# Layer-norm statistics of the first rows split over VectorE, ScalarE and GpSimd, other work moved behind or ahead

## The chip, the core and the metric

The kernel runs on one core of a Trainium2 chip. The time is device microseconds of one execution; a kernel is judged by the median of several. One more execution is profiled, and its trace gives what every engine did and when: TensorE (PE, its weight loads PEld), VectorE (DVE), ScalarE (ACT), GpSimd (POOL), SyncE (SP), which issues most of the DMAs.

## The reference

The input x has 2048 rows of 640. Each row is normalised (mean and variance over 640, eps 1e-5) to xn. Two branches read xn, and the result is x + s * g:

```python
x = A_x
xn = _layernorm(x, axis=-1)
s = _A_ref(xn, A_wq, A_wk, A_wv, A_wo, A_beta)   # attention, see below
g = _silu(_B_ref(xn, B_w_gate, B_w_up, B_w_down)) # (sigmoid(xn wg) * (xn wu)) wd
return x + s * g
```

The attention has 32 heads of 20 columns. The rows are cut in 4 segments of 512. Within a segment there is causal softmax attention; beside it stands a read from a memory matrix that sums phi(k) v over the earlier segments (phi(t) = t+1 for t > 0, else exp(t)), divided by its normaliser. Each head mixes the two by a gate sigmoid(beta), and wo projects the result. The gated branch has 1536 inner columns.

## The kernel before, in words

The whole program is written in one order by hand: each engine runs its instructions in the order in which the Python code emits them. A planner places the later work in 20 slots a segment; `at` and `later` give it due times. The change touches `startup`, which runs ahead of the slots, and what it calls.

In `startup` (L573) the first segment's 512 rows are taken in 4 blocks of 128 rows. Their DMAs are issued on SP first (`x_first`, L137), two blocks to a tile `xt2`, mixed with the two halves of Wv; Wk and Wq follow, then blocks of the next segment and gate weights. For each block:

- `ln_stats` (L227): two `bn_stats` and one `bn_aggr` on VectorE give mean and variance; GpSimd adds eps and raises to the power -0.5 (L241, L242), which gives `rstd`.
- `ln_norm` (L248): VectorE writes `xn` = (x - mean) * rstd. In the first segment TensorE transposes it in five pieces into a PSUM tile `pT` (L260) and ScalarE copies that to `xnT` (L261). In the second segment a DMA issued on SP transposes (L263).

`v_tile(0, j, half)` (L356) multiplies block j's part of `xnT` by one half of Wv in five matmuls into `psv`; ScalarE copies the result to `va` (L280). Six of the eight value tiles of the first segment stand in `startup`. `k_chunk` and `q_chunk` (L282, L314) need all four blocks of `xnT`; each is five matmuls of 512 columns, copied by ScalarE, five of each. `warm` (L568) issues matmuls of the identity with itself, whose result nobody reads, ahead of the first transposes (WARM = 40) and between the first and the second (10).

All these PSUM tiles (wps, pT, psv, psk, psq, gp, up) come from one ring of three buffers (`dtile`, L114): the fourth tile waits until the first is read.

GpSimd's other work in `startup`: it makes `ident`, fills `KT[0]` with ones (L575), then behind the value tiles fills the ones columns of `va` (`v_ones`, L192), builds the indicator `nInd` (`make_ind`, L196) and fills `KT[1]` and `KT[2]` (L593, L596). Key chunks read `nInd` at L305.

Keys and queries are staged to DRAM and come back in another layout: `stage_out` (L308) writes, `relay` (L271) issues four DMAs on SP that read the rows of half the heads into `KT` or `QT`. `relay(0, 1, Ks, KT)` (L630) brings the first segment's second half of key rows; the scores of slot 10 and later read them. `load_glu(i, which)` (L161) loads a third of the gate or up weights.

Of the kernel before, what the change touches and what calls it, by code (L numbers as in the profile page):

```python
# [9 lines left out]
P = 128  # L10
S = 2048
D = 640
# [17 lines left out]
ACT = mybir.ActivationFunctionType  # L30
ALU = mybir.AluOpType
# [18 lines left out]

NU = len(UNITS)
NSLOT = NG // 2 * NU
WARM = 40
FIRST = 0.45
PASS = [0.41, 0.41, 0.41, 0.2, 0.61]
R = NSLOT / 24
# [3 lines left out]
def kernel(  # L60
# [14 lines left out]
    nc = tc.nc  # L75
# [3 lines left out]
    cpool = ctx.enter_context(tc.tile_pool(name="const", bufs=1))  # L79
# [3 lines left out]
    lnp = ctx.enter_context(tc.tile_pool(name="ln", bufs=2))  # L83
    xpool = ctx.enter_context(tc.tile_pool(name="xpool", bufs=2))
# [44 lines left out]
    st = [dict() for _ in range(NSEG)]  # L129
# [31 lines left out]
    def load_glu(i, which):  # L161
        w, src = ((Wg, B_w_gate), (Wu, B_w_up))[which]
        nc.sync.dma_start(w[i][:], src[:, i * L:(i + 1) * L].rearrange("(c p) n -> p c n", p=P))
# [11 lines left out]

    nhalf = cpool.tile([P, 2], F32, name="nhalf")
    nc.gpsimd.memset(nhalf[:], -0.5)
    ident = cpool.tile([P, P], BF, name="ident")
    nc.gpsimd.memset(ident[:], 0.0)
    nc.gpsimd.affine_select(out=ident[:], in_=ident[:], compare_op=ALU.not_equal, fill=1.0,  # L180
# [6 lines left out]
    KT = [cpool.tile([P, 4, L], BF, name=f"KT{i}") for i in range(3)]  # L187
# [4 lines left out]
    def v_ones(a, b):  # L192
        for i in range(a, b):
            nc.gpsimd.memset(V[i][:, :, DH:VW], 1.0)
# [32 lines left out]
    def ln_stats(n, p, i0=0, i1=2):  # L227
        s = st[n]
        x = s[f"x{p}"]
        if i0 == 0:  # L230
            s[f"mv{p}"] = lnp.tile([P, 2, 2], F32, name="mv")
            s[f"rstd{p}"] = lnp.tile([P, 2], F32, name="rstd")
        mv, rstd = s[f"mv{p}"], s[f"rstd{p}"]
        for i in range(i0, i1):
            bs = lnp.tile([P, 2, 6], F32, name="bs")
            nc.vector.bn_stats(bs[:, 0, :], x[:, i, 0:HB])
            nc.vector.bn_stats(bs[:, 1, :], x[:, i, HB:D])
            nc.vector.bn_aggr(mv[:, i, :], bs[:])

        def root():  # L240
            nc.gpsimd.tensor_scalar(rstd[:, i0:i1], mv[:, i0:i1, 1], EPS, None, op0=ALU.add)  # L241
            nc.gpsimd.tensor_tensor(rstd[:, i0:i1], rstd[:, i0:i1], nhalf[:, i0:i1], op=ALU.pow)  # L242
        if n <= 1:
            root()
        else:
            later(0.6, root)

    def ln_norm(n, p, i):  # L248
# [4 lines left out]
        nc.vector.tensor_scalar(xn[:], s[f"x{p}"][:, i, :], s[f"mv{p}"][:, i, 0:1], s[f"rstd{p}"][:, i:i + 1],  # L253
                                op0=ALU.subtract, op1=ALU.mult)
        j = 2 * p + i
        dst = s["xnT"][:, :, j * P:(j + 1) * P]
        if n == 0:
            pT = dtile([P, DC, P], BF, "pT")
            for c in range(DC):
                nc.tensor.transpose(pT[:, c, :], xn[:, c * P:(c + 1) * P], ident[:])  # L260
            nc.scalar.copy(dst, pT[:])  # L261
        elif n == 1:
            nc.sync.dma_start_transpose(dst, xn[:])  # L263
        else:
            later(0.7, lambda: nc.sync.dma_start_transpose(dst, xn[:]))
# [5 lines left out]
    def relay(n, half, src, dst):  # L271
        rows = src[n % 2].rearrange("(g r d) n -> r d g n", r=4, d=DH)
        for r in range(4):
            nc.sync.dma_start(half_tile(dst, n, half)[32 * r:32 * r + DH, :, :], rows[r][:, 4 * half:4 * half + 4, :])
# [81 lines left out]
    def v_tile(n, j, half):  # L356
        s = st[n]
        ps = dtile([P, HB], F32, "psv")
        for k in range(DC):
            nc.tensor.matmul(ps[:], lhsT=s["xnT"][:, k, j * P:(j + 1) * P],  # L360
                             rhs=W["v"][:, k, half * HB:(half + 1) * HB],
                             start=(k == 0), stop=(k == DC - 1))
        va = V[4 * (n % 2) + j]
        evacuate(va[:, half * 16:(half + 1) * 16, 0:DH], ps[:].rearrange("p (h e) -> p h e", e=DH))
# [203 lines left out]
    def warm(count):  # L568
        ps = dtile([P, L], F32, "wps")
        for i in range(count):  # L570
            nc.tensor.matmul(ps[:, 0:P], lhsT=ident[:], rhs=ident[:], start=True, stop=True)

    def startup():  # L573
        warm(WARM)
        nc.gpsimd.memset(KT[0][:], 1.0)  # L575
        ln_stats(0, 0, 0, 1)
        ln_stats(0, 0, 1, 2)
        ln_norm(0, 0, 0)
        warm(10)
        ln_stats(0, 1, 0, 1)  # L580
        ln_norm(0, 0, 1)
        v_tile(0, 0, 0)
        ln_stats(0, 1, 1, 2)
        v_tile(0, 1, 0)
        ln_norm(0, 1, 0)
        v_tile(0, 0, 1)
        ln_norm(0, 1, 1)
        v_tile(0, 2, 0)
        v_tile(0, 1, 1)
        v_tile(0, 2, 1)  # L590
        v_ones(0, 4)
        make_ind()
        nc.gpsimd.memset(KT[1][:], 1.0)  # L593
        for c in range(DC):
            k_chunk(0, c)
        nc.gpsimd.memset(KT[2][:], 1.0)  # L596
        stage_out(0, 0, Ks, KT, "k5")
        for c in range(DC):
            q_chunk(0, c)
            if c == 0:  # L600
                stage_out(0, 1, Ks, KT, "k5")
                relay(0, 0, Ks, KT)
            elif c == 2:
                stage_out(0, 0, Qs, QT, "q5")
            if c < 2:
                ln_stats(1, 0, c, c + 1)
        make_bd()
        v_ones(4, 8)
        take(1)
        q_bound(0)  # L610
        relay(0, 0, Qs, QT)
        stage_out(0, 1, Qs, QT, "q5")
        c_in(0, (0,))
        load_glu(1, 0)
        load_glu(1, 1)
# [130 lines left out]
    n = NSEG - 1  # L746
# [39 lines left out]
```

## Time and profile before

| what | us |
|---|---|
| median of three runs | 339.98 |
| lowest and highest run | 338.81, 341.98 |
| profiled execution | 339.46 |
| span of its trace, first to last instruction | 337.70 |
| granted TensorE clock | 0.999 |
| first warm-up matmul starts | 1.45 |
| first key matmul starts | 12.42 |
| first scores start | 32.59 |

A timeline line reads: start and length in us, engine, source line, operation, output <- input, shapes, how many such instructions in a row were merged; in brackets the idle time of the engine ahead of it and what ended that. A line of a stage reads: the stage, its length, then busy time and number of instructions of each engine, the granted clock, the mean share of 16 DMA engines that was busy, and GB/s. Busy time of TensorE counts warm-up matmuls too.

### The profile page before, as it was taken

Reading aid. Unit: us, or ns where it says so; the run is one execution under the profiler, and the core shown is the slowest. Engines: PE = TensorE matmul, PEld = TensorE weight load, DVE = VectorE, ACT = ScalarE, POOL = GpSimd, SP = SyncE. Lnnn points to the kernel's source line nnn. Section 1 sums busy time; section 2 is a strip of 40 time slices with the busy share of each in tenths; the row PEclk is TensorE's granted clock in tenths of the full one; section 3 lists DMA queues with packets and bytes.
Section 4 is the critical chain, followed back from the end, with each engine's and each line's share of the span. In section 5 each row is a group of like instructions: output and inputs, shape, how many; then the busy total and the mean of one; then the engine's idle time right before and its main releaser. Section 6 shows DMA issues by size and latency. Waiting matters only on the chain.

```text
span 337.7 us, 8319 instructions
## 1 busy us (share of the span) xinstructions
PE 325.5 (96%) x3360; PEld 186.2 (55%) x3402; DVE 224.5 (66%) x533; ACT 225.8 (67%) x236; POOL 110.8 (33%) x157
## 2 busy tenths in 40 slices
PE   7999999999979999999999999999999999999995
PEld 7544455555654565554566466554456655544673
DVE  6375467579794677778777867875673687543355
ACT  3653897689766675377876675565887776786730
POOL 6645322232244222332235322332222323233214
PEclk9999999999999999999999999999999999999999
DMA  7956985667723621134730651042220521210032
GB/s 240 352 176 192 284 113 129 215 185 126 187 56 41 121 76 41 44 113 89 219 79 2 95 122 41 21 157 86 72 70 3 84 76 41 64 54 3 2 62 78
DMA packets 54725, 35.53 MB, mean 105 GB/s; under 512 B 28576, under 2 KB 54688, under 8 KB 54688
## 3 DMA queue, kind: packets, MB, share of 16 engines
q1 hardware_dynamic: 52480, 32.23, 37.6%
q10 hardware_dynamic: 2208, 2.79, 2.5%
q8 instruction: 26, 0.43, 0.6%
q14 instruction: 11, 0.09, 0.1%
HBM read 20.19 MB, written 8.39 MB: 85 GB/s over the span
## 4 chain that ended last, share of the span: by engine, by line
PE 82%; DVE 7%; DMA 4%; ACT 2%; issue 2%; SPq 1%; POOL 0%; DVEq 0%; ACTq 0%
PE up L438 14%; PE gp L428 14%; PE yp L456 11%; PE Aps L547 9%; PE Sps L522 7%; PE sp L502 6%; PE psv L360 6%; PE psk L289 6%; PE psq L321 6%; DMA Wu<-in_B_w_up_dram 2%; DMA Qs<-q 1%; ACT pt L527 1%; PE dm L388 1%; PE am L410 1%; DVE q L374 1%
## 5 line engine op out<-in xcount | busy, mean ns | idle before, releaser
L527 ACT ACTIVATE pt<-Sps 128x2048 bf16<-128x2048 f32 x80 | 150.1, 1876 | 26.1 <-PE Sps L522 23.7
L530 POOL TENSOR_SCALAR_AFFINE_SELECT pt<-pt 128x1024 bf16<-128x1024 bf16 (+1 forms) x80 | 75.7, 947 | 194.2 <-ACT pt L527 194.0
L438 PE MATMUL up<-xnT,Wu 128*128 128x512 bf16 x229 | 58.8, 379 | 0.8 <-DMA Wu<-in_B_w_up_dram 0.2
L428 PE MATMUL gp<-xnT,Wg 128*128 128x512 bf16 x221 | 58.0, 379 | 1.2 <-issue 0.2
L456 PE MATMUL yp<-Wd,hT 128*128 128x320 bf16 x384 | 57.1, 299 | 0.0
L442 DVE SCALAR_TENSOR_TENSOR hT<-tg,up 128x512 bf16<-128x512 bf16 x48 | 32.7, 682 | 35.0 <-PE up L438 30.3
L547 PEld LDWEIGHTS <-pt 128*128 128x128 bf16 x1280 | 43.3, 96 | 16.2 <-DVE od L556 3.4
L431 ACT ACTIVATE tg<-gp 128x512 bf16<-128x512 f32 x48 | 28.6, 597 | 34.3 <-PE gp L428 33.6
L547 PE MATMUL Aps<-va,pt 128*128 128x21 bf16 x1280 | 44.5, 173 | 2.6 <-DVE od L556 2.5
L456 PEld LDWEIGHTS <-hT 128*128 128x128 bf16 x384 | 35.3, 97 | 15.7 <-issue 2.8
L438 PEld LDWEIGHTS <-Wu 128*128 128x128 bf16 x240 | 21.3, 97 | 23.7 <-issue 2.4
L428 PEld LDWEIGHTS <-Wg 128*128 128x128 bf16 x240 | 21.0, 97 | 21.8 <-issue 1.9
L522 PE MATMUL Sps<-QT,KT 24*128 24x128 bf16 (+3 forms) x512 | 31.8, 301 | 0.9 <-ACT pt L527 0.5
L461 DVE SCALAR_TENSOR_TENSOR aa<-t,yp 128x320 bf16<-128x320 bf16 x32 | 15.4, 481 | 23.3 <-ACT t L459 23.2
L459 ACT ACTIVATE t<-yp 128x320 bf16<-128x320 f32 x32 | 14.0, 436 | 20.1 <-PE yp L456 19.0
L360 PE MATMUL psv<-Wv,xnT 128*128 128x320 bf16 x160 | 26.4, 300 | 0.1
L502 PE MATMUL sp<-Wo,oT 128*128 128x320 bf16 x160 | 25.9, 300 | 0.0
L321 PE MATMUL psq<-xnT,Wq 128*128 128x512 bf16 x96 | 23.6, 380 | 0.6 <-issue 0.5
L289 PE MATMUL psk<-xnT,Wk 128*128 128x512 bf16 x92 | 23.5, 380 | 0.3
L522 PEld LDWEIGHTS <-KT 24*128 24x128 bf16 x512 | 9.4, 92 | 25.3 <-issue 24.0
L504 DVE SCALAR_TENSOR_TENSOR aa<-aa,sp 128x320 bf16<-128x320 bf16 x32 | 15.5, 484 | 9.6 <-PE sp L502 9.5
L502 PEld LDWEIGHTS <-oT 128*128 128x128 bf16 x160 | 14.5, 98 | 8.1 <-issue 2.0
(74 smaller groups left out, 327.0 us busy)
## 6 DMA issues: line engine op xcount, KB each, us to landing
KT<-Ks SPq DMA_DIRECT2D x32, 80.0 KB
QT<-Qs SPq DMA_DIRECT2D x32, 80.0 KB
xr<-in_A_x_dram SPq DMA_DIRECT2D x15, 160.0 KB
out_dram<-xr SPq DMA_DIRECT2D x15, 160.0 KB
xt<-in_A_x_dram SPq DMA_DIRECT2D x6, 320.0 KB
Wg<-in_B_w_gate_dram SPq DMA_DIRECT2D x3, 640.0 KB
Wu<-in_B_w_up_dram SPq DMA_DIRECT2D x3, 640.0 KB
Wd<-in_B_w_down_dram ACTq DMA_DIRECT2D x1, 1920.0 KB
```

What stands on the lines that cost most here:

```text
L289: nc.tensor.matmul(ps[:], lhsT=W["k"][:, k, c * P:(c + 1) * P], rhs=s["xnT"][:, k, :], start=(k == 0), stop=(k == DC - 1))
L321: nc.tensor.matmul(ps[:], lhsT=W["q"][:, k, c * P:(c + 1) * P], rhs=s["xnT"][:, k, :], start=(k == 0), stop=(k == DC - 1))
L360: nc.tensor.matmul(ps[:], lhsT=s["xnT"][:, k, j * P:(j + 1) * P], rhs=W["v"][:, k, half * HB:(half + 1) * HB], start=(k == 0), stop=(k == ...
L428: nc.tensor.matmul(gp[:], lhsT=Wg[f // 4][:, k, fo:fo + P], rhs=s["xnT"][:, k, :], start=(k == 0), stop=(k == DC - 1))
L438: nc.tensor.matmul(ps[:], lhsT=Wu[f // 4][:, k, fo:fo + P], rhs=s["xnT"][:, k, :], start=(k == 0), stop=(k == DC - 1))
L442: empty(lambda: nc.vector.scalar_tensor_tensor(out=h[:], in0=tg[:], scalar=1.0, in1=ps[:], op0=ALU.add, op1=ALU.mult))
L456: nc.tensor.matmul(yp[:], lhsT=s["hT"][f][:, j * P:(j + 1) * P], rhs=W["d"][:, f, hs], start=(f == 0), stop=(f == FC - 1))
L502: nc.tensor.matmul(sp[:], lhsT=s["oT"][:, j, c, :], rhs=W["o"][:, c, hs], start=(c == 0), stop=(c == DC - 1))
L522: nc.tensor.matmul(Sps[:, r, c0:c0 + ncol], lhsT=kt[32 * r:32 * r + KR, gi, kb * P:(kb + 1) * P], rhs=qt[32 * r:32 * r + KR, gi, kb * P:L] ...
L527: nc.scalar.activation(pt[:], Sps[:], ACT.Exp, scale=SCALE)
L530: nc.gpsimd.affine_select(out=diag, in_=diag, compare_op=ALU.is_ge, fill=0.0, base=0, pattern=[[0, 4], [0, cnt], [1, P]], channel_multipli ...
L547: nc.tensor.matmul(A[:, qb, r, :], lhsT=pt[:, r, off:off + P], rhs=V[4 * (n % 2) + kb][:, 4 * g + r, :], start=first, stop=True, skip_grou ...
```

## The change

Five things:

- Two constants are added: `epsb` (eps in each partition) and a scratch `scr`. WARM goes from 40 to 34.
- The statistics of the first four blocks get functions of their own. Blocks 0, 2 and 3 keep `bn_stats` and `bn_aggr` on VectorE (`half_stats`, one half of a row at a time). For block 1 ScalarE sums the row by a copy with a sum output (`sum_act`), turns it into the negative mean, and sums the squares of x minus mean (`square_act`). The roots of blocks 0 and 1 are a Sqrt on ScalarE, followed by a reciprocal on VectorE; those of blocks 2 and 3 stay on GpSimd (`root_pool`). `norm_first` replaces `ln_norm` for this segment.
- The order in `startup` is another one: block 2's first half is taken between block 0's statistics and its normalisation, the value tiles come as (0,0), (0,1), transposes of block 2, (1,0), (1,1), transposes of block 3, (2,0), (2,1).
- A Sqrt on one column stands first on ScalarE; an Exp on one column stands behind the value tiles. On GpSimd a copy of one column of the last `xn` stands ahead of `v_ones`, `make_ind` and the fills of `KT[1]` and `KT[2]`.
- `relay(0, 1, Ks, KT)` is issued ahead of the two transposing DMAs of the second segment and of `load_glu(2, ...)`, not behind them.

```diff
-WARM = 40
+WARM = 34
...
+    epsb = cpool.tile([P, 1], F32, name="epsb")
+    nc.gpsimd.memset(epsb[:], EPS)
+    scr = cpool.tile([P, 2], F32, name="scr")
...
+    def half_stats(j, h):
+        s = st[0]
+        if h == 0:
+            s[f"bs{j}"] = lnp.tile([P, 2, 6], F32, name="bs")
+            s[f"mv{j}"] = lnp.tile([P, 2], F32, name="mv0", bufs=4)
+            s[f"r{j}"] = lnp.tile([P, 1], F32, name="r0", bufs=4)
+        nc.vector.bn_stats(s[f"bs{j}"][:, h, :], s[f"x{j // 2}"][:, j % 2, h * HB:(h + 1) * HB])
+        if h:
+            nc.vector.bn_aggr(s[f"mv{j}"][:], s[f"bs{j}"][:])
+
+    def root_act(j):
+        s = st[0]
+        nc.scalar.activation(s[f"r{j}"][:], s[f"mv{j}"][:, 1:2], ACT.Sqrt, bias=epsb[:])
+
+    def root_pool(j):
+        r = st[0][f"r{j}"][:]
+        nc.gpsimd.tensor_scalar(r, st[0][f"mv{j}"][:, 1:2], EPS, None, op0=ALU.add)
+        nc.gpsimd.tensor_tensor(r, r, nhalf[:, 0:1], op=ALU.pow)
+
+    def sum_act(j):
...
+        s["sq"] = fpool.tile([P, D], BF, name="aa", bufs=4)
+        s["sm"] = lnp.tile([P, 2], F32, name="sm", bufs=1)
...
+        nc.scalar.activation(s["sq"][:], s[f"x{j // 2}"][:, j % 2, :], ACT.Copy, accum_out=s["sm"][:, 0:1])
+
+    def square_act(j):
+        s = st[0]
+        nc.scalar.activation(s["sm"][:, 1:2], s["sm"][:, 0:1], ACT.Copy, scale=-1.0 / D)
+        nc.scalar.activation(s["sq"][:], s[f"x{j // 2}"][:, j % 2, :], ACT.Square, bias=s["sm"][:, 1:2],
+                             accum_out=s[f"mv{j}"][:, 1:2])
+        nc.scalar.activation(s[f"r{j}"][:], s[f"mv{j}"][:, 1:2], ACT.Sqrt, scale=1.0 / D, bias=epsb[:])
+
+    def norm_first(j):
...
+        r = s[f"r{j}"][:]
+        if j < 2:
+            nc.vector.reciprocal(r, r)
+        xn = lnp.tile([P, D], BF, name="xn")
+        mean, op = (s["sm"][:, 1:2], ALU.add) if j == 1 else (s[f"mv{j}"][:, 0:1], ALU.subtract)
+        nc.vector.tensor_scalar(xn[:], s[f"x{j // 2}"][:, j % 2, :], mean, r, op0=op, op1=ALU.mult)
+        pT = dtile([P, DC, P], BF, "pT")
+        for c in range(DC):
+            nc.tensor.transpose(pT[:, c, :], xn[:, c * P:(c + 1) * P], ident[:])
+        nc.scalar.copy(s["xnT"][:, :, j * P:(j + 1) * P], pT[:])
+        return xn
...
     def startup():
+        nc.scalar.activation(scr[:, 0:1], epsb[:], ACT.Sqrt)
         warm(WARM)
         nc.gpsimd.memset(KT[0][:], 1.0)
-        ln_stats(0, 0, 0, 1)
-        ln_stats(0, 0, 1, 2)
-        ln_norm(0, 0, 0)
+        sum_act(1)
+        half_stats(0, 0)
+        half_stats(0, 1)
+        root_act(0)
+        square_act(1)
+        half_stats(2, 0)
+        norm_first(0)
         warm(10)
-        ln_stats(0, 1, 0, 1)
-        ln_norm(0, 0, 1)
+        half_stats(2, 1)
+        root_pool(2)
+        norm_first(1)
         v_tile(0, 0, 0)
-        ln_stats(0, 1, 1, 2)
+        half_stats(3, 0)
+        half_stats(3, 1)
+        root_pool(3)
+        v_tile(0, 0, 1)
+        norm_first(2)
         v_tile(0, 1, 0)
-        ln_norm(0, 1, 0)
-        v_tile(0, 0, 1)
-        ln_norm(0, 1, 1)
+        v_tile(0, 1, 1)
+        xn = norm_first(3)
         v_tile(0, 2, 0)
-        v_tile(0, 1, 1)
         v_tile(0, 2, 1)
+        nc.gpsimd.tensor_copy(scr[:, 1:2], xn[:, 0:1])
+        nc.scalar.activation(scr[:, 0:1], epsb[:], ACT.Exp)
         v_ones(0, 4)
...
         load_glu(1, 1)
+        relay(0, 1, Ks, KT)
         ln_stats(1, 1, 0, 1)
...
         load_glu(2, 1)
-        relay(0, 1, Ks, KT)
         relay(0, 1, Qs, QT)
```

More of the change, by code (lines that the diff above doesn't have):

```diff
@@ L246, in ln_stats @@
             later(0.6, root)
+    def half_stats(j, h):
[18 more added lines that the diff above has]
+        s["sm"] = lnp.tile([P, 2], F32, name="sm", bufs=1)
+        s[f"mv{j}"] = lnp.tile([P, 2], F32, name="mv0", bufs=4)
+        s[f"r{j}"] = lnp.tile([P, 1], F32, name="r0", bufs=4)
+        nc.scalar.activation(s["sq"][:], s[f"x{j // 2}"][:, j % 2, :], ACT.Copy, accum_out=s["sm"][:, 0:1])
+    def square_act(j):
+        s = st[0]
+        nc.scalar.activation(s["sm"][:, 1:2], s["sm"][:, 0:1], ACT.Copy, scale=-1.0 / D)
[3 more added lines that the diff above has]
+    def norm_first(j):
+        s = st[0]
+        if j == 0:
+            s["xnT"] = xpool.tile([P, DC, L], BF, name="xnT")
+        r = s[f"r{j}"][:]
[9 more added lines that the diff above has]
+        return xn
     def ln_norm(n, p, i):
@@ L256, in ln_norm @@
         dst = s["xnT"][:, :, j * P:(j + 1) * P]
[L257 to L262, printed above, removed]
+        if n == 1:
             nc.sync.dma_start_transpose(dst, xn[:])
```

## The prediction

> **What bounds the kernel now.** I read the page first, then busy time by stage, then the first 13 us in order of time, and last the SP queue around 30 us.
>
> ```profile
> span 337.7 us, 8319 instructions
> PE 325.5 (96%) x3360; PEld 186.2 (55%) x3402; DVE 224.5 (66%) x533; ACT 225.8 (67%) x236; POOL 110.8 (33%) x157
> ```
>
> TensorE carries the span. The change touches only work before 12.4 us, and one group of DMA issues near 30 us, so the stages decide:
>
> ```profile
> core 0: us, PE busy (x) PEld busy (x) DVE busy (x) ACT busy (x) POOL busy (x), PEclk, DMA share, GB/s
> 0.00:12.42 12.42, 10.68 (x100) 8.79 (x101) 6.03 (x16) 6.00 (x10) 9.17 (x25) 1.00 0.87 275
> 12.42:32.59 20.17, 20.07 (x97) 8.74 (x97) 12.18 (x31) 9.32 (x17) 10.17 (x25) 1.00 0.66 210
> ```
>
> From 12.42 us, the first key matmul, TensorE has 0.10 us idle in 20.17. Whatever starts that matmul earlier moves everything behind it, if the weights are there; whatever does not is worth nothing. In the first 12.42 us "busy" misleads: 50 of the matmuls are warm-up (wps) and pay for nothing. In order of time:
>
> ```profile
> 4.13 0.44 DVE L236 BATCH_NORM_STATS2 bs<-xt 128x6 f32<-128x320 bf16 x1
> 5.23 0.45 DVE L253 TENSOR_SCALAR xn<-xt,mv,rstd 128x640 bf16<-128x640 bf16 x1
> 6.63 0.39 DVE L253 TENSOR_SCALAR xn<-xt,mv,rstd 128x640 bf16<-128x640 bf16 x1
> 7.08 0.45 PE L260 MATMUL pT<-ident,xn 128*128 128x128 bf16 x5 [0.18 <-DVE xn L253]
> 7.37 1.80 PE L360 MATMUL psv<-Wv,xnT 128*128 128x320 bf16 x10
> 8.31 0.52 PEld L360 LDWEIGHTS <-xnT 128*128 128x128 bf16 x5 [0.44 <-ACT xnT L261]
> 9.00 0.44 PE L260 MATMUL pT<-ident,xn 128*128 128x128 bf16 x5
> 9.06 0.66 POOL L194 MEMSET va<- 128x32 bf16 x4
> 9.15 0.89 DVE L253 TENSOR_SCALAR xn<-xt,mv,rstd 128x640 bf16<-128x640 bf16 x1 [0.77 <-POOL rstd L242]
> 9.28 0.84 PE L360 MATMUL psv<-Wv,xnT 128*128 128x320 bf16 x5
> 10.09 0.45 PE L260 MATMUL pT<-ident,xn 128*128 128x128 bf16 x5
> 10.38 2.20 PE L360 MATMUL psv<-Wv,xnT 128*128 128x320 bf16 x15
> 12.42 0.81 PE L289 MATMUL psk<-xnT,Wk 128*128 128x512 bf16 x2
> ```
>
> VectorE runs without a gap from 3.09 us to the second xn (ends 7.02): statistics of blocks 0 and 1, xn 0, statistics of block 2, xn 1. That xn releases the second transposes at 7.08. From there TensorE has 3 transpose groups and 6 value tiles. The last 15 value matmuls run 10.38 to 12.42, 0.136 us each, so 0.68 a tile; a transpose group takes 0.28 until the next work (9.00 to 9.28). The work is 6 x 0.68 + 3 x 0.28 = 4.92 us; the stage took 12.42 - 7.08 = 5.34. The other 0.42 is stalls: about 0.27 where tile (1,0) waits for ScalarE's copy of block 1 (8.31), and 0.13 ahead of the last transposes, whose xn took 0.89 us beside GpSimd's memsets instead of 0.39 to 0.45.
>
> **Part 1: second block's statistics on ScalarE, two roots there.** VectorE loses two bn_stats and one bn_aggr, 4.13 to 5.21, about 1.0 us of its chain; it gains two [128,1] reciprocals. The nearest row, a reciprocal of 128x16, is 0.25 us; I take 0.2, bounds 0.1 and 0.25. ScalarE's chain is not in the trace. Block 1 lands between 3.1 (block 0 seen at 3.09) and 4.13 (its statistics started without a wait); its DMA is issued 0.44 us after block 0's, 160 KB at 333 GB/s is 0.49, so 3.6. Then: copy with a sum, 0.69 as the copy xnT row; root of block 0, 0.23 as the tanh of 128x32 (L218); a small copy 0.2; square with a sum 0.69 to 0.8; root 0.23 to 0.3. No row shows what the sum output adds: between 0 and 0.25 us each, the top being the cost of one more small instruction; I take 0.1. Sum: 3.6 + 0.8 = 4.4, root 0 at 4.65, small copy 4.85, square to 5.8, root 1 to 6.15. Reciprocal to 6.4, xn 1 at 6.45 against 6.63 before: 0.16 earlier at the transposes (6.92). With 0.25 per sum it would be 0.13 later instead; with none, and a reciprocal of 0.1, 0.4 earlier.
>
> The root of block 0 waits behind the block-1 copy on ScalarE: ready at 4.22, it starts near 4.4. VectorE puts half of block 2's statistics there; block 2 lands about 4.1 to 4.5 (one more 160 KB at the 150 to 220 GB/s of 3.5 to 4.5 us), so they end by 5.0 at worst and xn 0 starts at 5.0 to 5.2, not after 5.23. The copy of xnT 0 comes behind the second root: pT 0 is ready near 6.05, so it runs 6.2 to 6.9 (before 6.37 to 7.06). Nobody is late.
>
> **WARM 40 to 34, and the extra memset.** 40 matmuls took 4.18 us of weight loads, so 34 end about 0.63 earlier, at 5.1; xn 0 ends near 5.45, so TensorE idles 0.3 us there. [...]
>
> **Part 2: order of value tiles.** (0,0), (0,1), transposes 2, (1,0), (1,1), transposes 3, (2,0), (2,1). Starting at 6.92: tile (0,0) 7.20, (0,1) 7.88, transposes 8.56, (1,0) 8.84, (1,1) 9.52, transposes 10.20, (2,0) 10.48, (2,1) 11.16, end 11.84. Each need: second half of Wv by 7.88 (bytes ahead of and with it 1.47 MB, by the GB/s of half-microsecond stages moved by 7.0, plus the 0.5 us between block 0's last byte and its reader); xn 2 at 8.4; xnT 1 at 8.15 for 8.84; xn 3 at 9.4 for 10.20; xnT 2 at 9.8 for 10.48; Wk (2.29 MB, moved by 9.2) for 11.84. The three buffers of the d ring come free in time, tightest that of (0,0), by 10.25 for 10.48. So no stall is left: 0.42 gained.
>
> **Part 3: GpSimd's fills behind xn 3.** xn 3: statistics end about 7.88, root 1.06 as before (8.06 to 9.12), xn 9.0 to 9.4 against 9.15 to 10.04. But in the new order transposes 3 come at 10.20, so even a 0.89 us xn would hide: worth 0 on the path. The fills take 0.66 + 1.25 + 3.6 and end near 15 instead of 14.18; nInd is read at 19.42, the KT tiles by DMAs near 30. The new wait (a copy of one column of xn 3) holds on GpSimd the fills and, behind them, only the roots of 21.14; nInd has 7.8 us to spare (19.42 less about 11.6), the rest more.
>
> **Part 4: table loads.** The page of before has one ACT_TABLE_LOAD, 1283 ns, at 0.78 us. The root moves another set ahead of it (hidden before 3.1 us) and the Exp at the end adds one load behind the last value copy, 12.47 to 13.75, then 0.23 of Exp. The first key copy, due at 13.12, runs 13.98 to 14.56; its buffer is wanted again by the fourth key chunk at 11.84 + 3 x 1.08 = 15.08. Hidden, with 0.52 us over; a load longer by more than that is on the path.
>
> [...]
>
> **Part 5: four KT relays ahead of the transposes.** The SP queue now:
>
> ```profile
> 30.65 3.56 SPq L263 DMA_TRANSPOSE xnT<-xn  x2
> 34.26 0.58 SPq L163 DMA_DIRECT2D Wg<-in_B_w_gate_dram  x1
> 34.90 1.00 SPq L163 DMA_DIRECT2D Wu<-in_B_w_up_dram  x1
> 35.99 1.64 SPq L274 DMA_DIRECT2D KT<-Ks  x4
> ```
>
> They pass two transposes and two weight loads, which are issued about 1.5 us later. Readers: value tiles of the second segment at 41.81 (no wait shown), gate 8 at 53.5, and KT's second half at slot 10, over 60 us. Cost 0 to the path; gain 0 too, since nobody waits for KT. The neighbour with a wait is Wu block 1: TensorE stood 0.24 us for it at 36.23. Without transposes right behind it that may go (-0.24), or the relays' 0.33 MB share its bandwidth (rival B). I take 0.
>
> **Sum.** 0.16 + 0.42 = 0.58 us, bounds 0.2 and 0.9. The profiled execution took 339.46 us, its span 337.70 and 1.76 around it; it becomes 338.9. It lay 0.52 under the median 339.98 of the three runs, which becomes 339.4.
>
> **Rivals.** [...] *B: the relays delay Wu.* 0.33 MB at the 344 to 371 GB/s of 32 to 34 us is 0.9 us; TensorE waits that much more at 36 us: 339.8, median 340.3. For it: the wait is there already; against: they are issued behind Wu. [...] *D: more table loads.* If Square is not in the root's set, two loads, 2.57 us, stand ahead of xn 1: start of the stage 9.5, end 14.4, median 342. *E: ScalarE is no quicker*: it does not bring xn 1 forward and the new order only partly pays, 0 to 0.2 gained, median 339.9.
>
> **Numbers.** Forecast 0.56, E 0.15, A 0.12, B 0.08, C 0.06, D 0.03. The range runs from the lowest run less the best gain (338.81 - 0.9 = 337.9) to the highest run less the forecast (341.98 - 0.58 = 341.4); it takes in A, B, C and E. About 1% (3.4 us) is what a measurement can tell from no change: no case reaches it alone, so faster 0.02, same 0.95, slower 0.03.
>
> **What would show it.** First key matmul near 11.8; xn 1 near 6.45; no wait of a value tile for xnT; a second ACT_TABLE_LOAD near 12.5 with no TensorE gap before 16; xn 3 at 0.4 us; no longer wait at Wu near 35.6. Wrong if xn 1 starts after 6.63, if a fill or DMA takes the place of the stalls, or if the key chunks stop.

## The result, and the profile after

The changed kernel takes 344.42 us in the median (343.11 to 346.56, six runs), the one before 339.43 (338.61 to 341.98, six runs, the three of the start among them): a ratio of 1.014, with a 95% interval of 1.0105 to 1.0174. That is 4.8 us slower (3.6 to 5.9), against 0.6 faster forecast, and above the top of the range, 341.4. Ratios, here and below, leave out single executions that took over 1.5% more than the fastest of the same kernel; medians hold all. The profiled execution took 343.11 us against 339.46.

The page of the changed kernel begins so:

```profile
span 341.4 us, 8315 instructions
PE 326.0 (95%) x3354; PEld 185.8 (54%) x3396; DVE 221.8 (65%) x532; ACT 229.5 (67%) x246; POOL 109.4 (32%) x155
```

TensorE has 0.5 us more of busy time in 3.7 us more of span: most of the time is idle time. First the startup, in order of time (start, length, engine, line, operation, output <- input, in brackets the idle time ahead of it and what ended it):

```profile
3.60 0.74 ACT L276 ACTIVATE aa<-xt 128x640 bf16<-128x640 bf16 x1 [1.33 <-DMA xt<-in_A_x_dram]
...
4.25 0.19 ACT L276 ACTIVATION_READ_ACCUMULATOR aa<-xt 128x1 f32 x1
...
4.75 0.83 ACT L281 ACTIVATE aa<-xt,sm 128x640 bf16<-128x640 bf16 x1
4.78 0.49 DVE L257 BATCH_NORM_STATS2 bs<-xt 128x6 f32<-128x320 bf16 x1 [0.59 <-DMA xt<-in_A_x_dram]
...
6.53 0.45 DVE L294 TENSOR_SCALAR xn<-xt,sm,r 128x640 bf16<-128x640 bf16 x1
...
9.10 0.45 DVE L294 TENSOR_SCALAR xn<-xt,mv,r 128x640 bf16<-128x640 bf16 x1 [0.77 <-POOL r L268]
```

ScalarE sums block 1 from 3.60 us, each sum output costs one more instruction of 0.19, and xn 1 starts at 6.53. The fourth xn takes 0.45 us, no longer 0.89. The same view for TensorE alone, and below it for ScalarE alone:

```profile
8.68 0.44 PE L297 MATMUL pT<-ident,xn 128*128 128x128 bf16 x5
8.96 1.52 PE L408 MATMUL psv<-Wv,xnT 128*128 128x320 bf16 x10
10.32 0.44 PE L297 MATMUL pT<-ident,xn 128*128 128x128 bf16 x5
10.60 1.52 PE L408 MATMUL psv<-Wv,xnT 128*128 128x320 bf16 x10
11.96 1.24 PE L337 MATMUL psk<-xnT,Wk 128*128 128x512 bf16 x4
```

```profile
12.60 1.28 ACT L648 ACT_TABLE_LOAD   x1
13.90 0.20 ACT L648 ACTIVATE scr<-epsb 128x1 f32<-128x1 f32 x1
14.01 1.05 ACT L328 CAST k<-psk 128x512 bf16<-128x512 f32 x2
```

No value tile waits, the first key matmul starts at 11.96 instead of 12.42, and the second table load is hidden: the first key copy starts at 14.01 and TensorE does not stop. At the first scores the changed kernel is 0.47 us ahead (32.12 against 32.59). What comes then, on TensorE:

```profile
35.32 0.40 PE L570 MATMUL Sps<-QT,KT 24*128 24x128 bf16 x8
38.77 1.48 PE L486 MATMUL up<-xnT,Wu 128*128 128x512 bf16 x5 [3.06 <-DMA Wu<-in_B_w_up_dram]
40.04 0.63 PE L595 MATMUL Aps<-va,pt 128*128 128x21 bf16 x16
40.52 2.29 PE L476 MATMUL gp<-xnT,Wg 128*128 128x512 bf16 x5
42.74 0.54 PE L570 MATMUL Sps<-QT,KT 24*128 24x256 bf16 x8
```

and the same place in the kernel before:

```profile
36.23 1.25 PE L438 MATMUL up<-xnT,Wu 128*128 128x512 bf16 x5 [0.24 <-DMA Wu<-in_B_w_up_dram]
37.33 0.56 PE L547 MATMUL Aps<-va,pt 128*128 128x21 bf16 x16
37.73 1.24 PE L428 MATMUL gp<-xnT,Wg 128*128 128x512 bf16 x5
38.91 0.40 PE L522 MATMUL Sps<-QT,KT 24*128 24x256 bf16 x8
```

The wait for the second third of Wu grew from 0.24 to 3.06 us, though its DMA was issued earlier (29.55 against 30.03). Behind it the same five gate matmuls take 2.29 us, not 1.24. Busy time by stage says why (PEclk, third from the end, is the granted clock):

```profile
core 0: us, PE busy (x) PEld busy (x) DVE busy (x) ACT busy (x) POOL busy (x), PEclk, DMA share, GB/s
...
36.00:37.00 1.00, 0.00 (x0) 0.00 (x0) 0.00 (x0) 1.00 (x2) 0.00 (x0) 1.00 0.70 138
37.00:38.00 1.00, 0.00 (x0) 0.00 (x0) 0.00 (x0) 0.79 (x1) 0.15 (x1) 1.00 1.24 101
...
40.00:41.00 1.00, 1.00 (x19) 0.68 (x18) 0.65 (x2) 0.00 (x0) 0.00 (x0) 0.50 1.07 344
41.00:42.00 1.00, 1.00 (x4) 0.35 (x3) 0.81 (x3) 0.00 (x0) 0.00 (x0) 0.50 1.09 343
42.00:43.00 1.00, 1.00 (x10) 0.14 (x8) 0.04 (x1) 0.15 (x1) 0.00 (x0) 0.50 1.10 353
```

While TensorE stood, the DMAs moved 101 to 138 GB/s, against 343 to 353 a little later; so all DMAs together moved far less than they do elsewhere. What held Wu back, the experiments have to show. After the gap TensorE runs at half clock for some 3 us (0.50 in the stages from 40 to 43 us). A second, smaller stall stands near 65 us, seen on VectorE:

```profile
64.92 0.69 DVE L326 CAST k<-psk 128x512 bf16<-128x512 f32 x1 [4.00 <-DMA pkt<-k]
```

The transposing DMA that this copy waits for was issued at 58.48 and landed at 64.80, 6.3 us later, beside the 1.9 MB load of the down weights. Before, it took 2.4 us (54.51 to 56.93), though the load was issued close behind it there too. The two issues on their queues, first before, then after:

```profile
54.51 1.20 SPq L378 DMA_TRANSPOSE pkt<-k  x1
54.76 1.33 ACTq L173 DMA_DIRECT2D Wd<-in_B_w_down_dram  x1
```

```profile
58.48 1.19 SPq L426 DMA_TRANSPOSE pkt<-k  x1
58.69 0.44 ACTq L173 DMA_DIRECT2D Wd<-in_B_w_down_dram  x1
```

Before, the load's issue lasted 1.33 us and ended behind the transpose's; after, it lasted 0.44 us and ended ahead of it. TensorE loses 1.02 us there, ahead of dm.

The account of the two profiled executions, by marks that both have: at the first scores -0.47; at the up matmuls +2.54 (38.77 against 36.23); at the scores behind them +3.83 (42.74 against 38.91: 1.29 more for the half clock); behind dm +5.11 (71.05 against 65.94); at the end +3.7, chiefly because a later wait for od fell from 2.1 to 1.1 us.

### The profile page after: what moved, and what is told of

Its sections match the earlier page's. It is cut to its first block, busy times and chain, and to the rows that moved or that the text cites. A ratio compares the mean times of both kernels' runs of the same rounds, so it can differ in the third digit from the quotient of the medians.

```text
span 341.4 us, 8315 instructions
## 1 busy us (share of the span) xinstructions
PE 326.0 (95%) x3354; PEld 185.8 (54%) x3396; DVE 221.8 (65%) x532; ACT 229.5 (67%) x246; POOL 109.4 (32%) x155
## 4 chain that ended last, share of the span: by engine, by line
PE 79%; DVE 8%; DMA 6%; ACT 2%; issue 2%; SPq 1%; POOL 0%; DVEq 0%; ACTq 0%
PE up L486 14%; PE gp L476 13%; PE yp L504 12%; PE Aps L595 8%; PE Sps L570 6%; PE sp L550 6%; PE psv L408 5%; PE psk L337 5%; PE psq L369 5%; DMA Wu<-in_B_w_up_dram 3%; DMA pkt<-k 2%; PE dm L436 1%; PE am L458 1%; ACT pt L575 1%; DVE k L422 1%
## 5 line engine op out<-in xcount | busy, mean ns | idle before, releaser
L476 PE MATMUL gp<-xnT,Wg 128*128 128x512 bf16 x221 | 59.0, 384 | 1.4 <-issue 0.2
```

The costliest lines, as they stand in the source:

```text
L476: nc.tensor.matmul(gp[:], lhsT=Wg[f // 4][:, k, fo:fo + P], rhs=s["xnT"][:, k, :], start=(k == 0), stop=(k == DC - 1))
```

## The experiments

Two theories. **T1:** the four relays alone make the loss, because the transposing DMAs behind them are late and Wu's landing is reported only then. **T2:** their bytes delay Wu (rival B of the prediction, at a higher price). Beside them stood the question whether the startup gains anything. All kernels, with the wait for Wu, half clock behind a gap, and the wait ahead of dm as their one profile shows them; ratios are to the kernel before, run beside them. One profile is one execution: kernels that are the same up to this place show 0.24 and 0.89 us of wait (the one before and e11_before_wd), 3.06 and 2.41 (the changed one and e9_after_wd), so differences of some 0.6 us in that column say nothing:

| kernel | median us (runs) | ratio, 95% interval | Wu wait | half clock | dm wait |
|---|---|---|---|---|---|
| e1_relay_back | 339.93 (10) | 0.9996, 0.9957 to 1.0035 | 0.7 | no | 1.1 |
| e2_relay_alone | 343.90 (10) | 1.0101, 1.0065 to 1.0138 | 2.9 | yes | none |
| e3_relay_between | 342.93 (10) | 1.0070, 1.0027 to 1.0112 | none | no | none |
| e4_turns_last | 344.31 (4) | 1.0126, 1.0049 to 1.0203 | 1.2 | not here; at 104 us | 1.0 |
| e5_half | 343.25 (4) | 1.0117, 1.0078 to 1.0157 | 2.0 | yes | 1.1 |
| e6_load_between | 341.74 (9) | 1.0059, 1.0029 to 1.0089 | 1.8 | yes | 1.2 |
| e7_filler | 346.01 (4) | 1.0148, 1.0084 to 1.0213 | 0.9 | not here; behind dm | 4.7 |
| e8_early | 343.68 (4) | 1.0116, 1.0096 to 1.0136 | none | yes, behind the scores | 1.2 |
| e9_after_wd | 342.54 (12) | 1.0094, 1.0062 to 1.0125 | 2.4 | yes | none |
| e10_back_wd | 338.75 (12) | 0.9989, 0.9953 to 1.0025 | none | no | none |
| e11_before_wd | 339.35 (12) | 1.0000, 0.9979 to 1.0021 | 0.9 | no | none |
| e12_back_wd_load | 339.62 (12) | 0.9997, 0.9967 to 1.0028 | 0.3 | no | none |
| e13_even | 341.88 (10) | 1.0072, 1.0035 to 1.0109 | 0.7 | no | 0.9 |
| e14_between_wd | 340.26 (10) | 1.0029, 0.9994 to 1.0063 | 0.2 | no | none |
| e15_between_look | 339.06 (1) | single run | 0.2 | no | none |
| e16_ten | 344.14 (4) | 1.0160, 1.0083 to 1.0236 | 3.3 | yes | none |

### Which part: the relays taken back, and the relays alone

The changed kernel with the relays in their old place:

```diff
         load_glu(1, 1)
-        relay(0, 1, Ks, KT)
...
         load_glu(2, 1)
+        relay(0, 1, Ks, KT)
         relay(0, 1, Qs, QT)
```

> The changed kernel with the four KT relays of the second half back in their old place, behind the transposes and the third weight loads. Theory (the relays make Wu block 1 land late, at 38.8 us, and the rest follows): TensorE's wait for Wu falls from 3.1 us to about 0.2, the clock stays at 1.0 between 39 and 43 us, and the median is 339.0, some 0.4 below the kernel before, the startup's own gain. Rival (the startup's edits shift the phase and the DMAs collide whatever the relays' place): the wait stays above 2 us and the median is 343 to 345.

The median is 339.93: the whole loss is gone. But it is 0.9 us above the expected value, and no gain over the kernel before is left; the profile has the stall ahead of dm (1.06 us) and 0.7 us each for Wg and Wu. Now the kernel before, with nothing but the relays moved (the opposite edit there):

> The kernel before with nothing but the relays moved ahead of the transposes. Theory: Wu lands 2.5 to 3 us later than 36.2, TensorE waits about 3 us and then runs at half clock for some 3 us, median 344 to 345. Rival (the startup's edits): median 339.4, wait 0.2.

```profile
39.21 1.46 PE L438 MATMUL up<-xnT,Wu 128*128 128x512 bf16 x5 [2.87 <-DMA Wu<-in_B_w_up_dram]
40.45 0.63 PE L547 MATMUL Aps<-va,pt 128*128 128x21 bf16 x16
40.93 2.29 PE L428 MATMUL gp<-xnT,Wg 128*128 128x512 bf16 x5
```

TensorE's timeline of this kernel shows the same wait and the same slow matmuls as the changed one. The median rises by 4.1 us (343.90 against 339.76). So the relays are the cause, with or without the new startup.

### Why: four DMAs of the same bytes, in two shapes

In the trace the landing of a DMA is a group of increments of its semaphore, here called reports: Wu shows sixteen, a relay ten. Whatever sends one of them is called a ring here; the trace does not name it. Two kernels settle what the difference does. Both are the kernel before with four extra DMAs of 80 KB between Wu and the transposes, whose data nobody reads: once over 128 partitions,

```diff
         load_glu(1, 1)
+        for r in range(4):
+            nc.sync.dma_start(QT[2][:, r, 0:320], Ks[0][r * P:(r + 1) * P, 0:320])
```

> The kernel before with four more DMAs of 80 KB between Wu block 1 and the two transposes; each spreads over 128 partitions (640 bytes each) instead of the 20 partitions (4 x 1 KB each) of a relay; their data is not used. Theory (a relay holds only ten of the rings, and the transpose, with Wu's last reports, waits for those ten): with all sixteen sharing the bytes evenly, 0.33 MB at 357 GB/s is 0.9 us, so TensorE waits for Wu 0.9 to 1.5 us, no half clock follows, and the median is 340 to 341.5. Rival (bytes or the mere number of DMAs between Wu and the transposes): a wait of 2.5 to 3 us as with the relays, half clock, and 343 to 344.5.

and once over 20, as a relay has them:

```diff
         load_glu(1, 1)
+        rows = Ks[0].rearrange("(g r d) n -> r d g n", r=4, d=DH)
+        for r in range(4):
+            nc.sync.dma_start(QT[2][32 * r:32 * r + DH, :, :], rows[r][:, 4:8, :])
```

> The control of the even spread: the kernel before with four more DMAs in the same place and of the same 80 KB, in the form of a relay, 20 partitions each; their data is not used, and the real relays stay where they were. Theory and rival both: a wait for Wu of 2.5 to 3.1 us, half clock behind it, 343 to 345; if it is as short as with the even spread, the theory of the ten rings falls.

TensorE's timeline, first with the even shape, then with 20 partitions:

```profile
36.89 1.25 PE L438 MATMUL up<-xnT,Wu 128*128 128x512 bf16 x5 [0.68 <-DMA Wu<-in_B_w_up_dram]
37.98 0.56 PE L547 MATMUL Aps<-va,pt 128*128 128x21 bf16 x16
38.39 1.24 PE L428 MATMUL gp<-xnT,Wg 128*128 128x512 bf16 x5
```

```profile
39.60 1.45 PE L438 MATMUL up<-xnT,Wu 128*128 128x512 bf16 x5 [3.33 <-DMA Wu<-in_B_w_up_dram]
40.84 0.63 PE L547 MATMUL Aps<-va,pt 128*128 128x21 bf16 x16
41.32 2.29 PE L428 MATMUL gp<-xnT,Wg 128*128 128x512 bf16 x5
```

Same bytes, same number, same place: 0.68 against 3.33 us, the shorter of them no longer than the kernel before can show. T2 falls: the bytes alone do not make the wait. The even shape still costs 2.4 us in the median, a little above the 340 to 341.5 expected, with less wait for Wu than expected: the transposes are late too, so that value tiles of the second segment wait 1.1 us for xnT, and dm waits 0.9. The times of the single reports, read from the traces (us from the start of each span):

```
kernel            Wu, second third: its 16 reports        next on its rings        that one's reports   first transpose
before            36.09-36.19                             transpose                                     36.70-36.80
e3_relay_between  35.02-35.10                             transpose                                     35.63-35.73
e10_back_wd       35.56-35.64                             transpose                                     36.18-36.28
after             ten 34.69-37.24, six 38.67-38.72        relays on ten of 16      last: 38.69-38.82    39.26-39.41
e2_relay_alone    ten 35.43-37.73, six 39.12-39.16        relays on ten of 16      last: 39.15-39.18    39.70-39.88
e16_ten           ten 35.26-37.91, six 39.52-39.56        20 partitions, ten       last: 39.55-39.59    40.11-40.29
e13_even          35.37-36.84                             128 partitions, all 16   last: 37.75-37.81    38.56-39.90
e12_back_wd_load  35.77-37.14                             Wg, third third          39.06-39.17          39.72-39.80
```

Wherever in these rows a DMA stands directly ahead of a transposing one on a ring, its report from that ring comes in the same tenth of a microsecond as those from the other such rings (36.09 to 36.19 before), mostly 0.6 us ahead of the transpose's own (36.70 to 36.80). Where Wu is followed by an ordinary DMA on all of its rings, its reports come one by one over 1.4 us or more (35.77 to 37.14 in e12_back_wd_load, 35.37 to 36.84 in e13_even). In the changed kernel ten of Wu's reports come one by one up to 37.24, and the other six, as many as a relay leaves out, together at 38.67 to 38.72, beside the last relay's (38.69 to 38.82). The reading: on six rings, without a relay, the transpose follows Wu directly, and Wu's report waits until the ten others have worked off the relays. TensorE's up matmuls start at 38.77, 0.05 us behind the sixteenth report, and at 36.23 before, 0.04 behind it. So the six idle rings, not the ten busy ones, are last. That a transposing DMA holds back the report ahead of it is read from these rows; how the queue does it, no run shows.

The packets in the trace of the changed kernel fit: of the first transpose's 640 packets (256 bytes each), 194 begin between 34.35 and 35.11 us, and the 640th at 38.70, together with Wu's last reports. So the transpose does not wait for all sixteen rings to begin, as the expectation of e5_half below has it: on some rings, most likely the six without relays, it was under way more than 3 us ahead of the reports. Late there are the reports, then, and probably not Wu's data; the packets do not name their rings, so this is not shown ring by ring.

Two things differ between the shapes and were not taken apart. A relay gives ten reports, not sixteen, and its bytes also take longer: the middle reports of one DMA and the next lie 0.5 to 0.7 us apart with 20 partitions, 0.3 with 128. In the rows above the late reports are six wherever DMAs of 20 partitions stand between, so the first goes with which reports are held; the second may go with how long.

### Other places for the relays, the transposes and the loads

Relays behind the transposes, ahead of the third gate load:

```diff
         load_glu(1, 1)
-        relay(0, 1, Ks, KT)
...
         ln_norm(1, 0, 1)
+        relay(0, 1, Ks, KT)
```

> The changed kernel with the relays behind the two transposes and ahead of the third weight loads. If it is the relays' place right behind Wu, ahead of the transposes, that matters: wait for Wu 0.2 us and 339 us. If it is that relays stand anywhere ahead of the third weight loads: a later wait (the weights of chunk 8) and over 341 us.

The wait for Wu is gone, and the profiled execution is the quickest of its ten runs, 338.14 us. Yet the median is 342.93: three runs lie between 338.1 and 340.8, seven between 342.3 and 344.8. A single further execution was to profile one of the longer ones:

> The changed kernel with the relays behind the transposes and ahead of the third gate block, once more, for a profile. Seven of its ten runs took 342 to 345 us: if this one does, its profile shows where the 4 us go. Expected by the theory of the collision: a wait of DVE for pkt of about 4 us near 62 us, and no wait for Wu at 36. By the rival, that the relays delay the third gate or up block: a wait for Wg or Wu near 50 us.

It took 339.06 us and shows neither stall, so what the longer runs lose remains unseen. What both profiles do show is a new wait of TensorE, for xnT at the second segment's value tiles near 50 us: 1.1 us in the first, 1.3 in this one.

The two transposes taken away from behind Wu and issued behind the third loads, the relays left early:

```diff
+    turns = []
+
     def ln_norm(n, p, i):
...
-            nc.sync.dma_start_transpose(dst, xn[:])
+            turn = lambda: nc.sync.dma_start_transpose(dst, xn[:])
+            if p == 0:
+                turns.append(turn)
+            else:
+                turn()
...
         load_glu(2, 1)
+        for turn in turns:
+            turn()
```

> The changed kernel, relays where the change puts them, with the two transposing DMAs of blocks 0 and 1 of the second segment issued behind the third weight loads. If the late part of Wu is the part that runs beside the transposes (the rows of 35 to 38 us move only 91 to 138 GB/s): wait for Wu under 0.7 us, 339 to 340 us, perhaps a wait of the second segment's value tiles near 41 us. If the relays alone take the bandwidth, or if all DMAs in flight share it: wait 1 to 3 us, over 341 us.

Missed: the wait for Wu fell only to 1.2 us (its reports, with no transpose behind, came at 35.63 to 37.51), and xnT became late instead, with 1.2 us of waiting at the value tiles. There is no half clock here (1.00 from 38 to 44 us), but one at 104 us, behind a wait of 2.1 us for od. The third Wu, now directly ahead of a transpose, gave all its reports at 43.73 to 43.85.

Two of the four relays early (`relay` with a range of r, 0 to 2 early and 2 to 4 in the old place):

> The changed kernel with two of the four relays early and two back in their old place. Theory (the transposes run only when all 16 DMA rings have come to them; the relays, 20 partitions each, hold ten of the rings, at 0.65 us a relay in the changed kernel's landings, and what stands directly ahead of a transpose on the other rings reports its landing only then): two relays less are 1.3 us less, Wu lands near 37.4 instead of 38.7 and TensorE waits 1.5 to 2.0 us; the gap is too short for the half clock, median 340.5 to 342. Rival (any relay ahead of the transposes costs the same): wait about 3 us, 344.

The wait is 2.0 us, the top of what was expected, though Wu's last report came at 38.47 us, not 37.4. The median of 343.25 is above what was expected; the profile shows half clock behind this gap too (0.50 from 40 to 43 us), and dm waits 1.1 us.

The third gate load between the relays and the transposes:

```diff
         relay(0, 1, Ks, KT)
+        load_glu(2, 0)
...
-        load_glu(2, 0)
         load_glu(2, 1)
```

> The changed kernel with the load of the third gate weights, which uses all 16 rings, issued between the relays and the transposes. Theory (the landing of Wu is held back on the rings where a transpose stands directly behind it): the six late reports come with the others, Wu lands between 35.3 and 37.3, TensorE waits 1.5 us or less; no half clock; 341 to 342.5, as the later transposes may cost a wait near 44. Rival (bandwidth: more bytes in flight make Wu later still): wait over 3 us, 345.

The median falls to 341.74, inside the expected range, but the wait and the half clock are not as expected. Fifteen of Wu's reports come early, at 35.90 to 36.48, as the theory says; one ring comes at 38.52, and TensorE waits 1.8 us for it. What held that ring is not known. The same load ahead of the transposes without early relays, and with the edit of the down weights below (`load_glu(2, 0)` directly behind `load_glu(1, 1)`):

> As the one with the relays back and Wd later, and the third gate weights issued between the second up weights and the transposes. Theory (the DMA directly ahead of a transpose reports its landing only with the transpose): Wu lands 35 to 36 us, no wait of TensorE for it (0.24 to 0.7 before), no half clock; the transposes land about 2 us later, near 39.5, ahead of the value tile that reads them at 41: median 338.3 to 338.8, the best of all. Rival (bandwidth: the extra load shares it with Wu, or the value tiles wait): 339.5 or more.

Missed, 339.62: Wu no longer waits long (0.3 us), but xnT does, as the view of waits shows (engine, line, what it waited for: us in total, times, longest):

```profile
PE psv L408 <- DMA xnT<-xn: 1.8, 1, 1.8
...
PE up L486 <- DMA Wu<-in_B_w_up_dram: 0.3, 1, 0.3
```

Loading the weights of both middle blocks at the start instead (`load_glu(1, 0)` and `load_glu(1, 1)` behind the first `load_glu(0, 1)`):

> The changed kernel with both second weight loads issued at the start, behind the first ones (near 10 us instead of 29), the relays where the change puts them. Theory: the relays ahead of the transposes harm only through the weight load that stands on the rings with them; without it no wait for Wu, clock 1.0, and the startup's 0.4 us is seen: 338 to 339.2. Rival (the relays delay the transposes, and the value tiles or the later transposes pay): 341 or more. A cost of its own is possible: keys staged behind 1.3 MB more, first scores later than 32.1.

Missed, and by the cost it named: there is no wait for Wu, but the last rows of QT (read from Cs) come later behind the added bytes, and the first scores start at 35.09, not 32.12, with half clock from 36 to 39 us behind that gap:

```profile
35.09 1.38 PE L572 MATMUL Sps<-QT,KT 24*128 24x512 bf16 x4 [2.74 <-DMA QT<-Cs]
```

### The half clock

The changed kernel with 50 matmuls of `warm` ahead of the waiting up tile, so that TensorE does not stand:

```diff
         s = st[n]
+        if n == 0 and f == 4:
+            warm(50)
         ps = dtile([P, L], F32, "up")
```

> The changed kernel with 50 warm-up matmuls ahead of the matmuls that wait for Wu, nothing else. It leaves the late landing as it is and takes away TensorE's idle time ahead of it. Theory (part of the loss is the half clock of 39.8 to 43 us, which follows the idle 3 us): granted clock 1.00 throughout, the work from Wu to the third scores takes 2.7 us instead of 4.0, median 342.5 to 343.3. Rival (the clock dip is beside the point, or the fillers only push the wait): 344 or more.

The part that was to be shown is there: no half clock at this place (1.00 from 39 to 44 us), and the way from the up matmuls to the next scores takes 2.67 us, not 3.97.

```profile
37.15 2.96 PE L621 MATMUL wps<-ident 128*128 128x128 bf16 x50
41.01 1.25 PE L488 MATMUL up<-xnT,Wu 128*128 128x512 bf16 x4 [0.89 <-DMA Wu<-in_B_w_up_dram]
42.09 0.56 PE L597 MATMUL Aps<-va,pt 128*128 128x21 bf16 x16
42.51 1.24 PE L476 MATMUL gp<-xnT,Wg 128*128 128x512 bf16 x5
43.68 0.40 PE L572 MATMUL Sps<-QT,KT 24*128 24x256 bf16 x8
```

The time missed: 346.01. The profiled execution is the longest of four (349.61 us), and it loses more further on than the 1.3 us won here. VectorE's timeline shows where, at the wait for pkt beside the down weights:

```profile
69.42 0.69 DVE L326 CAST k<-psk 128x512 bf16<-128x512 f32 x1 [7.70 <-DMA pkt<-k]
```

TensorE stands 4.72 us there, ahead of dm, and runs at half clock until 74 us. Whether the other three executions lose as much there is not shown, so the filler's worth for the whole time stays open.

### The second stall: the down weights one slot later

```diff
-    at(6.8, 0, load_late, "d", B_w_down)
+    at(7.3, 0, load_late, "d", B_w_down)
```

In the changed kernel, in the one with the relays taken back, and in the kernel before:

> The changed kernel with the load of Wd (1.9 MB, issued on ScalarE) one slot later, so that the last transposing DMA of the first segment's keys is not issued 0.2 us ahead of it. Theory (in kernels with the new startup that transpose and Wd are in flight together: it lands 6.3 us after its issue instead of 2.4, the copies of the second segment's keys wait 4 us for it and TensorE 1.0): no wait of dm for k near 65 us, 1.0 to 1.3 us less than the changed kernel, median 343.2. Rival (that wait is only slack moved): 344.4, a new wait behind it. A cost: matmuls that read Wd could wait near 82 us.

> The relays back in their old place and Wd one slot later, the rest of the change as it is. Theory (the new startup starts the keys 0.25 to 0.5 us earlier, but loses 1.0 again to the key transpose that flies with Wd): no wait of dm, median 338.8 to 339.2, 0.5 to 1.0 below the kernel before with the same move. Rival (the earlier start is lost elsewhere whatever is done): 339.9.

> The kernel before with Wd one slot later and nothing else: the control. Its profile shows no wait for the key transposes, so theory says no change: 339.8, ratio 1.000 within 0.3%. If later Wd alone helps or harms (the executions of 342.5 at clock 0.995 would have to do with it), it is off that by 0.5 us or more.

No stall ahead of dm stands in any of the three profiles. Where there was one, the ratio to the kernel before falls from 1.0140 to 1.0094 and from 0.9996 to 0.9989; where there was none, nothing changes (1.0000). The intervals of the first two pairs overlap, so the stall is shown in the traces, and its price in the medians is not shown: it may be 0.5% in the changed kernel, and with the relays taken back it is next to nothing. VectorE's timeline of the second of them, at the copy that had waited 4.0 us for pkt:

```profile
60.16 0.69 DVE L326 CAST k<-psk 128x512 bf16<-128x512 f32 x1 [1.59 <-PE psk L337]
```

The expectations take it that the transpose is slow when it flies beside the load, and only with the new startup. All the traces together say something narrower. In eight of them the load's issue ended ahead of that transpose's issue, and the transpose landed after 5.7 to 10.0 us; one of the eight is the kernel before with the four even DMAs (5.7). In the other ten the load's issue ended later, and the transpose landed after 2.3 to 2.5 us; among them are the kernel before, the one with the relays alone and the one with four DMAs over 20 partitions, where the load's issue began 0.2 to 0.5 us behind the transpose's as well, but lasted 1.1 to 1.4 us. Why that issue is short in one kernel and long in another, no run shows.

The same edit together with the relays behind the transposes:

> The changed kernel with the relays behind the transposes and ahead of the third gate block, and with the down weights one slot later. If the pkt transposes' collision with the down weights' load makes the slow group of the kernel without that second edit (342 to 345 in 7 of 10 runs): 338 to 340 in nearly all runs. If something else does: still 342 to 344 in most runs.

The median is 340.26, between 339.23 and 342.85. The ratio is 1.0029, against 1.0070 with the earlier load, and the longer runs have mostly gone, three of ten still being over 341.5. That would fit a collision in the longer runs; but the intervals overlap (0.9994 to 1.0063, 1.0027 to 1.0112), and neither profile of the kernel with the earlier load shows one, so the cause stays open. This profile has the wait for xnT too, 1.9 us near 52 us.

## Why the prediction was wrong, step by step

- **Bound, and where the edit acts: right.** Most of the time went into TensorE's idle time in one stage that the prediction had named, ahead of the second third of Wu.
- **Part 5, "Cost 0 to the path": this is the step that failed.** It looked at the readers of what the relays pass, the transposes and the third weights, and found slack there (xnT was indeed not waited for). What the transposes do to the DMA ahead of them it touched in one clause ("without transposes right behind it that may go"), and drew a gain of 0.24 us from it at most: it did not see that, with four relays of ten reports between, Wu's other six reports come only at 38.67 to 38.72, 1.4 us behind the ten and 0.6 us ahead of the first transpose's (39.26 to 39.41). Rival B had the place and the direction, but as bandwidth: 0.9 us, and only 8 in 100, "against: they are issued behind Wu". The runs put in its place: Wu's landing, from issue to last report, grew from 6.16 to 9.17 us; the wait by 2.8; with the same bytes in an even shape the wait was 0.68, within what the kernel before itself can show (0.24 and 0.89). That DMAs issued behind a load cannot delay its landing was the wrong assumption.
- **No price on an idle TensorE.** The sum has no term for what an idle gap brings behind it. The gap at 36 us was followed by half clock at 40 to 43 us, 1.3 us more until the next scores; with the filler this part vanishes.
- **What a later DMA costs: not in the sum.** Beside the load of the down weights, the last pkt transpose takes 4 us longer to land than before. That adds 1.0 us ahead of dm in the changed kernel, and in the kernel with only the startup edits. It is no matter of a shifted start (0.25 us between the two issues before, 0.21 after); the load's issue was shorter, 0.44 against 1.33 us.
- **Part 1 (0.16): 0.10 measured at xn 1** (6.53 against 6.63), 0.05 at its transposes (7.03 against 7.08). Each sum output costs 0.19 us, near the upper bound of 0.25; the reciprocals 0.11 and 0.14. Block 2 landed at 4.78, later than the 4.1 to 4.5 taken, so xn 0 came 0.14 us later than before, not earlier; TensorE stood 0.59 us for it (0.3 forecast), off the path, since the next transposes wait for xn 1.
- **Part 2 (0.42): right**: no value tile waits, and with Part 1 the first key matmul starts 0.46 us earlier against 0.58. It does not always hold: where the second half of Wv came late, tile (0,1) waited 0.4 to 0.8 us (half of the relays, and the transposes last).
- **Part 3 (0), Part 4 (hidden): right.** The fourth xn takes 0.45 us and nobody waited for it; the load lasts 1.28 us and the first key copy starts at 14.01, 0.03 after the due time worked out.
- **Rivals A, C, D, E: none came.** One load more, no gap behind it; it starts at 12.60, as the copy ahead of it ends, and ends at 13.88, and the next instruction starts at 13.90, so the switch of tables cost its row and no more (A). The value matmuls of the startup run at a granted clock of 1.00 from 7.32 us (ten in 1.53), so no run shows a late clock there (C). The only load ahead of xn 1 is the one at 0.78 us (D), and the stage ends at 11.96 against 11.84 forecast.
- **What was left of 0.46 us:** the kernel with the relays back is at 0.9996, with the later down weights at 0.9989 (0.9953 to 1.0025). The startup's gain is in the trace; in the medians it cannot be told from nothing. No version measured here beats the kernel before beyond doubt.

Open remain the longer runs of the relays behind the transposes, the one late ring with the load between, and what makes the down weights' issue short or long, and with it the landing of the pkt transpose 6 or 2.4 us.

## What to carry to other kernels

When a DMA is moved on a queue, look at the DMAs on both sides of its new place, those issued ahead of it too. Here four relays of ten reports each, put between a load of sixteen that TensorE waited for and a transposing DMA, cost 4.1 us in the median (e2_relay_alone); it was the place to avoid. The same bytes with all rings alike cost less, but not nothing (2.4 us in e13_even, as the transposes were late). Waits of TensorE of 2.4 to 4.7 us were followed here by a clock of 0.50 for two to four us, which has to be priced with the wait; of those between 1.8 and 2.1 us some were and some were not. A change in one place can alter how two DMAs meet much later, as here the pkt transpose and the load of the down weights at 58 us, so a gain or loss has to be followed to the end of the span.

## What the runs showed of the hardware

- The reports of a DMA directly ahead of a transposing DMA came from all rings together: sixteen reports of Wu within 0.1 us against a spread of 1.5 us where an ordinary DMA follows on all rings (36.09 to 36.19 before; 35.37 to 36.84 in the even shape). With ten of the rings taken by relays, the other six reported 1.4 us behind the last of the ten (38.67 against 37.24). Reports close together alone do not tell this: the third gate load, right behind the transposes, has them too (43.77 to 43.89 with the relays alone).
- Idle gaps of TensorE of 2.4 us and more (2.4, 2.9, 3.1 and 3.3 ahead of the up matmuls, 2.7 ahead of the first scores, 4.7 ahead of dm) were each followed by two to four microseconds at a clock of 0.50; those of 1.3 and less were not. Between 1.8 and 2.1 both happened: half clock followed gaps of 1.8 (the load between), 2.0 (half of the relays) and 2.1 (the transposes last, at 104 us), full clock those of 1.8 and 1.9 near 52 us (e12_back_wd_load, e14_between_wd) and of 2.1 near 99 us (the kernel before, e10_back_wd). What decides it between 1.8 and 2.1 us, no run shows.
- A sum output on ScalarE showed as an instruction of its own, 0.19 us, behind a copy of 0.74 and a square of 0.83 us on 128x640 in the changed kernel.
- A transposing DMA on SP's queue landed after 5.7 to 6.5 us (10.0 with the filler: 59.28 to 69.30) where a 1.9 MB load's issue on ScalarE's queue ended ahead of the transpose's own, and after 2.3 to 2.5 us where it ended later.
